# Eighteen products of the identity with itself in the first chunk of a recurrent layer with two gated layers behind it

## The chip, the cores and the metric

The kernel runs on one core of a Trainium2 chip. The metric is the device time of one launch in microseconds (us), taken as the median of several runs. The engines are named as in the profile: PE is TensorE (PEld its weight loads), DVE is VectorE, ACT is ScalarE, POOL is GpSimd, SP is SyncE, which issues most of the transfers.

## The reference

Three layers follow each other. The first is a recurrence over 768 steps for 4 batches of 8 heads, with a 40x40 state per head; the other two are gated layers over the 3072 resulting rows of 320 numbers.

```python
for t in range(S):                       # B=4, H=8, S=768, D=40
    y[:, :, t] = einsum('bhd,bhde->bhe', rt, state)
    Sa = einsum('bhde,bhe->bhd', state, at)
    state = state * wt[:, :, None, :] - einsum('bhd,bhe->bhde', Sa, bt) \
            + einsum('bhd,bhe->bhde', vt, kt)
...
g = x @ w_gate                           # 3072 x 320 times 320 x 1536
x = (g * sigmoid(g)) * (x @ w_val) @ w_out
gate = sigmoid(x @ w2_gate)
x = gate * (x @ w2_val) @ w2_out
```

## The kernel before, in words

The recurrence is cut into 12 chunks of 64 steps. For a chunk the kernel scales its inputs by running products of the decay, multiplies keys with keys (`kps`), inverts a triangular 64x64 matrix for each of the 32 pairs of batch and head, carries the state through the chunk (`qps`, `ups`, `sps`), and forms the outputs (`aps`, `yps`). `prep_a` does the first two of these, `prep_b` the inverse, `chain` the state, `post` the outputs. The work of neighbouring chunks and the first gated layer of earlier chunks is mixed by `merge`, which draws from generators by fixed rates; a scheduler then sets the order of each engine's instructions from its own estimate of time. On the chip each engine works through its list.

In the first three chunks the inverse is built in steps by `halves`. Seven sums on DVE (L567 multiplies, L573 adds) give the inverses of 16-row blocks. A first group of 64 small products on PE (`hps`, L588) is copied by ACT (L596) and goes into a second group of 64 (L601). DVE and ACT copy that result into the matrix (L617, L615), DVE turns it (L619), and then `prep_b` does the last level with `zps` and `xps` (L647).

Two other strands run beside this. The first gated layer's weights come in pieces (`raw`). Each piece goes through ACT (L1008), POOL (L1011), four steps on DVE (L1014, L1015, L1019, L1020), a cast on ACT (L1030) and two or three steps on POOL (L1032 to L1038); pieces of 384 columns and of 320 follow each other. And `powers` makes the running products of the decay for chunks 4 to 7. DVE clamps the decays (L240), which is held back until the turned copy (L619) of chunk 1 is done; POOL then makes 21 steps (L237), 14 of them on `wp`. DVE takes the reciprocal of the last of these (L257), and POOL goes on with `wq`. The results go to memory and come back for chunk 4.

The first gated layer for chunk 0 starts as soon as three of its twelve weight slices are there. It writes its two products into one PSUM bank, `gv`. DVE multiplies them into `g` (L1117), and PE writes the bank again for the next slice only after that.

A matrix product of 32-bit floats is recorded as two matmuls, so a group that the order calls x4 is x8 in the trace; transposes are recorded once.

Of the kernel before, what the change touches and what calls it, by code (L numbers as in the profile page):

```python
# [9 lines left out]
F32 = mybir.dt.float32  # L10
# [4 lines left out]
ALU = mybir.AluOpType  # L15
AX = mybir.AxisListType
PSUM = bass.MemoryType.PSUM
DRAM = bass.MemoryType.DRAM
P = 128
# [20 lines left out]
F_HIGH = (1.875 - 2.0**-23) * 2.0**16  # L40


def attention(ctx, tc, st, ident, ins, banks, extra, early, more):

# [1 line left out]
    nc = tc.nc  # L48
# [6 lines left out]
    room, fills = {}, []  # L55
# [63 lines left out]
    def tied(mats, gates):  # L119
        for x, ys, c in [(mats[0], gates, "Sync"), *((x, mats[:1], "NoSync") for x in mats[1:])]:  # L120
            for y in ys:
                tc.add_manual_dep(
                    x.ins,
                    y.ins.name,
                    mybir.DependencyInfo(getattr(mybir.DependencyClass, c), mybir.DependencyReason.DATA),
                    reason="one group",
                )
# [90 lines left out]
    inv, done, out = {}, set(), {}  # L218
# [3 lines left out]
    groups = [list(range(x, y)) for x, y in zip(cuts, cuts[1:])]  # L222
# [57 lines left out]
    for hs in HALF:  # L280
        nc.gpsimd.affine_select(
            out=mask[hs, :],
# [263 lines left out]
    def halves(m, X, bn, ps):  # L546
        t = wk.tile([P, 32 * 32], F32, tag="sn", name="sn", bufs=1)
        full = t[:, 0:512].rearrange("p (t s) -> p t s", s=32)
        sn = t[:, 512:768].rearrange("p (t s) -> p t s", s=16)
        nt = t[:, 768:896].rearrange("p (t s) -> p t s", s=16)  # L550
        t = wk.tile([P, 15 * 2 * 30], F32, tag="pr", name="pr")
        pr, turned, zt = t, t[:, 0:512].rearrange("p (t q g) -> p t q g", q=NS, g=2), t[:, 512:768]
        zt = zt.rearrange("p (q r) -> p q r", r=16)
        nc.vector.transpose(out=full, in_=walk(bn[:], 0, (1, 16), (C, NS), (16, 2)))
        nc.scalar.mul(out=sn, in_=full[:, :, 0:16], mul=par[:, 0:1])
        nc.vector.scalar_tensor_tensor(
            out=sn, in0=full[:, :, 16:32], scalar=par[:, 1:2], in1=sn, op0=ALU.mult, op1=ALU.add
        )
        nk = sn.rearrange("p t s -> p (t s)")[:, 16:256:34]
        ev, od = sn[:, 0:16:2], sn[:, 1:16:2]  # L560
        nc.scalar.mul(out=x16.rearrange("p r t -> p (r t)")[:, 1:256:34], in_=nk, mul=-1.0)
        nc.vector.tensor_tensor(out=nt, in0=ev, in1=nk[:, :, None].to_broadcast([P, 8, 16]), op=ALU.mult)
        nc.vector.tensor_tensor(out=od, in0=od, in1=nt, op=ALU.add)
        for kk in range(1, 8):
            n = 2 * kk
            o = pr[:, 0 : 2 * n * n].rearrange("p (r u s) -> p r u s", u=2, s=n)
            nc.vector.tensor_tensor(  # L567
                out=o,
                in0=x16[:, 0:n, None, 0:n].to_broadcast([P, n, 2, n]),
                in1=sn[:, None, n : n + 2, 0:n].to_broadcast([P, n, 2, n]),  # L570
                op=ALU.mult,
            )
            nc.vector.tensor_reduce(out=x16[:, 0:n, n : n + 2], in_=o, axis=AX.X, op=ALU.add)  # L573
            if kk in (3, 5):
                yield
        rows = wk.tile([P, 16, NS, 2], F32, tag="x1t", name="x1t")
        flat = lambda x: x.rearrange("p a q g -> p (a q g)")
        nc.vector.transpose(out=flat(rows), in_=walk(x16[:], 0, (16, 16), (0, 2), (1, 16)))
        nc.vector.transpose(out=flat(turned), in_=walk(x16[:], 0, (1, 16), (0, 2), (16, 16)))
        for z in range(2):  # L580
            src = turned[:, :, :, z].rearrange("p t q -> p q t")
            to = lambda l: X[:, :, 32 * l + 16 * z : 32 * l + 16 * z + 16]
            nc.scalar.mul(out=to(1), in_=src, mul=sel[:, 2 + z : 3 + z])
            nc.vector.tensor_scalar(out=to(0), in0=src, scalar1=sel[:, z : z + 1], scalar2=None, op0=ALU.mult)
        yield
        for q in range(NS):
            for j in range(4):
                nc.tensor.matmul(  # L588
                    ps[QUAD[j], q, 0:16],
                    lhsT=bn[32 * j : 32 * j + 16, q, 0:32],  # L590
                    rhs=rows[32 * j : 32 * j + 16, :, q, 0],
                    start=True,
                    stop=True,
                    tile_position=(32 * j, 32 * j),
                )
        nc.scalar.copy(out=zt, in_=ps[:, :, 0:16])  # L596
        yield
        for q in range(NS):
            for j in range(4):
                at = 32 * (j % 2) + 16  # L600
                last = nc.tensor.matmul(  # L601
                    ps[32 * j : 32 * j + 16, q, 16:32],
                    lhsT=zt[QUAD[j], q],
                    rhs=X[QUAD[j], q, at : at + 16],
                    start=True,
                    stop=True,
                    tile_position=(32 * j, 32 * j),
                )
        if m == 0:
            marks["joined"] = last  # L610
        for j in (0, 2, 1, 3):
            at = 32 * (j % 2) + 16
            to, src = X[32 * j : 32 * j + 16, :, at : at + 16], ps[32 * j : 32 * j + 16, :, 16:32]
            if j % 2:
                nc.scalar.mul(out=to, in_=src, mul=-1.0)  # L615
            else:
                nc.vector.tensor_scalar(out=to, in0=src, scalar1=-1.0, scalar2=None, op0=ALU.mult)  # L617
        x1t = wk.tile([P, NS, 32], F32, tag="x1t", name="x1t")
        last = nc.vector.transpose(out=x1t, in_=walk(X[:], 0, (C, NS), (1, 32)))  # L619
        if m == 1:  # L620
            marks["turned"] = last
        yield x1t.rearrange("p q (r g) -> p r q g", g=2)

    def prep_b(m):
        X = xinv[m % 2]
        while m not in inv:
            yield
        bn = inv.pop(m)
        pool, tag = (po, f"po{m}") if m < 2 else (pmm, "mm")
        if m < FEW:  # L630
            ps = pool.tile([P, NS, 32], F32, tag=tag, name="hps")
            steps = halves(m, X, bn, ps)
        else:
            steps = whole(m, X, bn)
        for x1t in steps:
            yield

        zt = wk.tile([P, NS, 32], F32, tag="zt", name="zt")
        for n in range(2):
            ps = pool.tile([P, NS, 32], F32, tag=tag, name="zx"[n] + "ps")  # L640
            mats = []
            for q in range(NS):
                for h2 in range(2):
                    with group(m, not mats):
                        lo, hi = slice(64 * h2, 64 * h2 + 32), slice(64 * h2 + 32, 64 * h2 + 64)
                        mats.append(
                            nc.tensor.matmul(  # L647
                                ps[(hi, lo)[n], q],
                                lhsT=(bn[lo, q, 32:64], zt[hi, q])[n],
                                rhs=(x1t[lo, :, q], X[hi, q, 32:64])[n],  # L650
                                start=True,
                                stop=True,
                                tile_position=(64 * h2 + 32 * n, 64 * h2 + 32 - 32 * n),
                            )
                        )
            if m >= FEW:
                tied(mats, copied if n else [])
            copied = []
            for h2 in range(2):
                lo, hi = slice(64 * h2, 64 * h2 + 32), slice(64 * h2 + 32, 64 * h2 + 64)  # L660
                if n:
                    nc.scalar.mul(out=X[lo, :, 32:64], in_=ps[lo], mul=-1.0)
                else:
                    copied.append(nc.scalar.copy(out=zt[hi], in_=ps[hi]))
            yield
        if m == 0:
            marks["merged"] = mats[-1]
# [177 lines left out]
    def post(m):  # L845
# [4 lines left out]
        for bp in range(2):  # L850
# [49 lines left out]
                            )  # L900
            if m >= FEW:
                tied(mats, masked)
            ysb = wk.tile([P, DM + 64], F32, tag="ysb", name="ysb", bufs=3)
            yf, pf = yps.rearrange("p h d -> p (h d)"), pn[:, DM * bp : DM * bp + DM]
            freed[:] = [
# [418 lines left out]
def rwkv_moe_kernel(ctx, tc, r, k, v, w, a, b, aw0, aw, aa, akb, av, avt, art, w1a, w2a, out):  # L1324
# [11 lines left out]
    with ExitStack() as c1:  # L1336
# [8 lines left out]
        with ExitStack() as c2:  # L1345
# [10 lines left out]
            def more(new, spare):  # L1356
# [5 lines left out]
                for tag in new[:n]:  # L1362
                    tags.append(tag)
                    yield from ffn.load_w(st, tag, layers[0], len(w1))
                    w1.append(ffn.w)

            def fills(fs, after=None):
                for f in fs:
                    yield from ffn.load_w(*first[f], layers[0], f, after)
                    w1.append(ffn.w)  # L1370
# [13 lines left out]
                        nc.sync.dma_start(out=xs[1][2 * m + u], in_=ob)  # L1384
                        yield

            attention(c2, tc, st, ident, (aw0, aw, aa, akb, av, avt, art), banks, extra, fills, more)

        with ExitStack() as c2:
            pool2 = lambda n, b, **kw: c2.enter_context(tc.tile_pool(name=n, bufs=b, **kw))  # L1390
# [166 lines left out]
```

## Time and profile before

| | |
|---|---|
| time before, median of 3 runs | 1271.05 us (1270.66 to 1273.36) |
| the profiled execution | 1274.74 us |
| its span, first to last instruction | 1272.7 us |
| PE busy | 1185.2 us (93%) |
| PEld busy | 1070.1 us (84%) |
| DVE busy | 687.8 us (54%) |
| ACT busy | 592.3 us (47%) |
| POOL busy | 557.7 us (44%) |
| mean granted TensorE clock | 0.956 of full speed |

A granted clock of 1.00 is 2.4 GHz, and 0.50 is 1.2 GHz; a stretch with a value between has some of both. Times in the rows are from the start of the span. A row of the timeline gives start, length, engine, line, operation, what is written from what, shapes and count, and in brackets the idle time before it with what ended that.

### The profile page before, as it was taken

Reading aid. Unit: us, or ns where it says so; the run is one execution under the profiler, and the core shown is the slowest. Engines: PE = TensorE matmul, PEld = TensorE weight load, DVE = VectorE, ACT = ScalarE, POOL = GpSimd, SP = SyncE. Lnnn points to the kernel's source line nnn. Section 1 sums busy time; section 2 is a strip of 40 time slices with the busy share of each in tenths; the row PEclk is TensorE's granted clock in tenths of the full one; section 3 lists DMA queues with packets and bytes.
Section 4 is the critical chain, followed back from the end, with each engine's and each line's share of the span. In section 5 each row is a group of like instructions: output and inputs, shape, how many; then the busy total and the mean of one; then the engine's idle time right before and its main releaser. Section 6 shows DMA issues by size and latency. Waiting matters only on the chain.

```text
span 1272.7 us, 31392 instructions
## 1 busy us (share of the span) xinstructions
PE 1185.2 (93%) x12545; PEld 1070.1 (84%) x12545; DVE 687.8 (54%) x1432; ACT 592.3 (47%) x1447; POOL 557.7 (44%) x749
## 2 busy tenths in 40 slices
PE   5598799999999999899999999999999999999997
PEld 4487588889889988788898888888888888888886
DVE  6867769876678667956867544467121212121111
ACT  8465546556655575455433433445232323232222
POOL 5744842233223224356855766676232223222221
PEclk8678868999999999999999999999999999999998
DMA  7444664544655555343464543323010101000001
GB/s 221 131 131 148 146 168 123 123 99 111 153 121 115 115 136 122 88 106 110 125 237 126 182 160 127 107 88 91 2 46 1 46 1 35 1 21 1 22 1 25
DMA packets 180460, 124.38 MB, mean 98 GB/s; under 512 B 134608, under 2 KB 160208, under 8 KB 179536
## 3 DMA queue, kind: packets, MB, share of 16 engines
q1 hardware_dynamic: 180144, 122.11, 35.5%
q8 instruction: 101, 1.65, 0.5%
q14 instruction: 55, 0.45, 0.1%
q10 hardware_dynamic: 160, 0.16, 0.1%
HBM read 90.81 MB, written 31.43 MB: 96 GB/s over the span
## 4 chain that ended last, share of the span: by engine, by line
PE 60%; DVE 22%; ACT 8%; issue 4%; DMA 2%; POOL 2%; SPq 0%; DVEq 0%; ACTq 0%; POOLq 0%
PE g L1167 31%; PE po L1128 16%; DVE pr L526 4%; PE gv L1112 4%; DVE part L532 3%; PE kps L486 2%; PE aps L861 2%; PE tp L371 2%; DVE lq L498 1%; PE ups L787 1%; ACT bn L496 1%; DVE am L870 1%; DVE dt L1015 1%; ACT bn L495 1%; ACT part L751 1%
## 5 line engine op out<-in xcount | busy, mean ns | idle before, releaser
L1167 PE MATMUL g<-x,w 128*128 128x512 f32 (+1 forms) x1792 | 419.8, 385 | 2.1 <-DVE g L1174 2.0
L1167 PEld LDWEIGHTS g<-x,w 128*128 128x128 f32 x1792 | 323.3, 188 | 62.8 <-issue 2.8
L1176 POOL TENSOR_TENSOR hl<-g,hh 128x256 fp32r<-128x256 f32 x216 | 162.1, 756 | 281.8 <-ACT hh L1175 253.9
L1174 DVE TENSOR_TENSOR g<-g,g 128x256 f32<-128x256 f32 x216 | 82.1, 419 | 342.4 <-PE g L1167 340.1
L1128 PE MATMUL po<-w,hh 128*128 128x320 f32 x1152 | 233.6, 311 | 0.9 <-ACT hh L1118 0.8
L1128 PEld LDWEIGHTS po<-w,hh 128*128 128x128 f32 x1152 | 187.0, 188 | 9.9 <-ACT hh L1118 1.0
L1175 ACT CAST hh<-g 128x256 fp32r<-128x256 f32 x216 | 86.9, 406 | 179.4 <-PE po L1128 169.7
L1112 PE MATMUL gv<-x,w 128*128 128x256 f32 x1152 | 165.6, 291 | 3.8 <-DVE g L1117 2.5
L1128 PE MATMUL po<-w,hl 128*128 128x320 f32 x576 | 151.1, 313 | 3.6 <-POOL hl L1119 3.5
L1112 PEld LDWEIGHTS gv<-x,w 128*128 128x128 f32 x1152 | 147.7, 192 | 6.8 <-DVE g L1117 3.9
L1171 ACT ACTIVATE g<-g 128x256 f32<-128x256 f32 x216 | 73.0, 382 | 149.5 <-PE g L1167 143.1
L1119 POOL TENSOR_TENSOR hl<-g,hh 128x256 fp32r<-128x256 f32 x72 | 62.8, 872 | 128.8 <-ACT hh L1118 127.9
L1032 POOL TENSOR_TENSOR dt<-dt,w 128x384 f32<-128x384 f32 (+1 forms) x72 | 80.3, 1116 | 87.5 <-ACT w L1030 42.7
L1128 PEld LDWEIGHTS po<-w,hl 128*128 128x128 f32 x576 | 99.6, 188 | 5.6 <-POOL hl L1119 5.2
L498 DVE TENSOR_TENSOR lq<-kps,part 64x256 f32<-64x256 f32 x96 | 40.5, 422 | 85.9 <-ACT bn L496 67.0
L526 DVE TENSOR_TENSOR pr<-part,sn 128x4 f32<-128x4 f32 (+4 forms) x135 | 76.2, 565 | 3.7
L1014 DVE TENSOR_SCALAR dt<-dt 128x384 int32<-128x384 int32 (+1 forms) x72 | 41.8, 580 | 52.8 <-POOL dt L1011 52.5
L486 PE MATMUL kps<-lq,kbt 104*128 104x128 f32 x384 | 61.3, 309 | 8.9 <-DVE lq L498 6.4
L532 DVE TENSOR_REDUCE part<-pr 128x2 f32<-128x4 f32 (+4 forms) x135 | 66.6, 493 | 2.8
L486 PEld LDWEIGHTS kps<-lq,kbt 104*128 104x128 f32 x384 | 53.4, 215 | 13.2 <-PE yps L892 4.1
L861 PE MATMUL aps<-rbd,ut 104*128 104x128 f32 x384 | 57.1, 295 | 6.1 <-DVE ysb L906 3.6
L1030 ACT CAST w<-dt 128x384 fp32r<-128x384 f32 (+1 forms) x72 | 35.6, 495 | 55.3 <-DVE dt L1015 48.2
(185 smaller groups left out, 1711.4 us busy)
## 6 DMA issues: line engine op xcount, KB each, us to landing
raw<-in_w_dram SPq DMA_DIRECT2D x48, 384.0 KB
xd<-x SPq DMA_DIRECT2D x12, 896.0 KB
x<-xd SPq DMA_DIRECT2D x11, 896.0 KB
raw<-in_w_dram SPq DMA_DIRECT2D x24, 320.0 KB
ld<-in_a_kb_dram SPq DMA_DIRECT2D x22, 320.0 KB
ld<-rd SPq DMA_DIRECT2D x64, 80.0 KB
pn<-pd SPq DMA_DIRECT2D x32, 160.0 KB
ld<-in_a_a_dram SPq DMA_DIRECT2D x12, 320.0 KB
```

The lines of the kernel that those rows point to most:

```text
L486: nc.tensor.matmul(kps[:, n].rearrange("p h t -> p (h t)"), lhsT=kbt[0:PW, n, :], rhs=lq[m % 3][0:PW, 4 * g4 + n].rearrange("p h t -> p (h ...
L526: nc.vector.tensor_tensor(out=o, in0=xs[:, 0:kk, None, 0:n].to_broadcast([P, kk, 2, n]), in1=sn[:, None, n : n + 2, 0:n].to_broadcast([P, ...
L532: nc.vector.tensor_reduce(out=xs[:, 0:kk, n : n + 2], in_=o, axis=AX.X, op=ALU.add)
L861: nc.tensor.matmul(aps[:, n, h2], lhsT=ut[0:PW, x, 2 * h2 : 2 * h2 + 2].rearrange("p u s -> p (u s)"), rhs=rbd[0:PW, x, h2].rearrange("p b ...
L1032: sub(out=tf, in0=tf, in1=w.bitcast(F32), op=ALU.subtract)
L1112: nc.tensor.matmul(gv[n], lhsT=p, rhs=q, start=e == 0, stop=e == len(seq) - 1)
L1128: self.nc.tensor.matmul(ops[u], lhsT=p[:, us], rhs=q, start=first and n == 0, stop=last and n == 2)
L1167: nc.tensor.matmul(gv[k][:, 0:n], lhsT=p, rhs=cols(at), start=e == 0, stop=e == len(seq) - 1)
L1171: nc.scalar.activation(out=g[j], in_=gv[0][:, j], func=AF.Silu if silu else AF.Sigmoid)
L1174: nc.vector.tensor_tensor(out=g[j], in0=gv[1][:, j], in1=g[j], op=ALU.mult)
L1175: nc.scalar.copy(out=hh, in_=g[j])
L1176: self.heng.tensor_tensor(out=hl, in0=g[j], in1=hh.bitcast(F32), op=ALU.subtract)
```

## The change

A function `warm` is added. It issues n products of the 128x128 identity with four copies of itself side by side, which are 512 columns, into a fresh tile of the `gv` bank. Nothing reads them. The first is made to follow a given instruction, and each of the others the one before it. It is called at five places, all in chunk 0: eight products behind the fourth sum of `halves` (with a wait on DVE for that sum), three behind the first group of `hps`, two behind the second, one behind `zps`, and four behind the first `yps`.

```diff
+            red = nc.vector.tensor_reduce(out=x16[:, 0:n, n : n + 2], in_=o, axis=AX.X, op=ALU.add)
+            if m == 0 and kk == 4:
+                warm(red, 8, "Sync")
...
         nc.scalar.copy(out=zt, in_=ps[:, :, 0:16])
+        if m == 0:
+            warm(last, 3)
...
             marks["joined"] = last
+            warm(last, 2)
...
+            if n == m == 0:
+                warm(mats[-1], 1)
...
+            if m == bp == 0:
+                warm(mats[-1], 4)
...
+            def warm(inst, n, kind="NoSync"):
+                pool, tag = ffn.pg[0]
+                to = pool.tile([P, 4, P], F32, tag=tag, name="gv")
+                wide = ident[:, None, :].to_broadcast([P, 4, P])
+                with tc.high_priority(2000):
+                    for _ in range(n):
+                        mm = nc.tensor.matmul(to, lhsT=ident, rhs=wide, start=True, stop=True)
+                        tc.add_manual_dep(mm.ins, inst.ins.name, ...)
+                        inst, kind = mm, "NoSync"
```

The scheduler places these products and then lays out the rest anew, so other instructions move as well. In the changed kernel all lines behind the first edit have higher numbers: L588, L601, L647 are now L590, L605, L652; L617, L619 are L622, L624; L1014 to L1020 are L1023 to L1029; L1117 is L1126; the products are L1382.

On PE, around the inverse of chunk 0, the new list reads as follows (`gv<-ident` are the products, `tp` transposes of chunk 1's keys):

```order
L1382 MATMUL gv<-ident 128x512 x8
L590 MATMUL hps<-x1t,bn 32x16 x64
L1382 MATMUL gv<-ident 128x512 x3
L605 MATMUL hps<-part_212,pr 16x16 x64
L1382 MATMUL gv<-ident 128x512 x2
L371 MATMUL tp<-ident,tkb_90 104x128 x8
L652 MATMUL zps<-x1t,bn 32x32 x32
L1382 MATMUL gv<-ident 128x512
L486 MATMUL kps<-lq_210,kbt 128x128 x4
```

Without the four rows of products this is the list of before as well.

On DVE, at the same place, the list of before has the copy of the second group (`hps`) and its turn behind one weight piece of 384 columns (`dt_1453`) and ahead of the next (`dt_1490`):

```order
L1014 TENSOR_SCALAR dt_1453<-dt_1453 128x384
L1015 SCALAR_TENSOR_TENSOR dt_1453<-raw_1451,dt_1453 128x384
L1019 TENSOR_SCALAR ds_1454<-dt_1453 128x384
L1020 SCALAR_TENSOR_TENSOR ds_1454<-raw_1451,ds_1454 128x384
L617 TENSOR_SCALAR part1_212<-hps_325 16x16x16 x2
L619 STREAM_TRANSPOSE x1t_536<-part1_212 128x512
L1014 TENSOR_SCALAR dt_1490<-dt_1490 128x384
```

In the new list both pieces of 384 columns (`dt_1476`, `dt_1513`) stand ahead of them:

```order
L1023 TENSOR_SCALAR dt_1476<-dt_1476 128x384
L1024 SCALAR_TENSOR_TENSOR dt_1476<-raw_1474,dt_1476 128x384
L1028 TENSOR_SCALAR ds_1477<-dt_1476 128x384
L1029 SCALAR_TENSOR_TENSOR ds_1477<-raw_1474,ds_1477 128x384
L1023 TENSOR_SCALAR dt_1513<-dt_1513 128x384
L1024 SCALAR_TENSOR_TENSOR dt_1513<-raw_1511,dt_1513 128x384
L1028 TENSOR_SCALAR ds_1514<-dt_1513 128x384
L1029 SCALAR_TENSOR_TENSOR ds_1514<-raw_1511,ds_1514 128x384
L622 TENSOR_SCALAR part1_212<-hps_325 16x16x16 x2
L624 STREAM_TRANSPOSE x1t_552<-part1_212 128x512
```

The copy and the turn have moved behind four instructions of a weight piece.

On DVE, some 80 instructions later, the list of before goes from chunk 2's last key products (`lq2`) straight to chunk 2's inverse (`sn`) and to the first gated layer's `g`; the reciprocal (L257) stands 30 instructions further on:

```order
L498 TENSOR_TENSOR lq2_211<-kps_1362,part2_86 64x4x64 x2
L554 STREAM_TRANSPOSE sn_1838<-bn_1300 128x512
L418 TENSOR_TENSOR part0_88<-ld_1713,dtp_1725 128x8x2x32
L1117 TENSOR_TENSOR g_1642<-gv_1625,g_1642 128x256
L556 SCALAR_TENSOR_TENSOR sn_1838<-sn_1838,part2_86 128x256
```

In the new list the reciprocal of the last of POOL's `wp` stands ahead of them:

```order
L1079 TENSOR_TENSOR x_1628<-xtp_1636,x_1628 64x256
L498 TENSOR_TENSOR lq2_211<-kps_1385,part2_86 64x4x64
L257 RECIPROCAL part2_86<-wp_1506 128x40
L498 TENSOR_TENSOR lq2_211<-kps_1385,part2_86 64x4x64
L554 STREAM_TRANSPOSE sn_1861<-bn_1323 128x512
L556 SCALAR_TENSOR_TENSOR sn_1861<-sn_1861,part2_86 128x256
L1126 TENSOR_TENSOR g_1665<-gv_1648,g_1665 128x256
```

The reciprocal has moved ahead of chunk 2's inverse and of the first `g`.

## Rows read from the trace of the kernel before

**Rows 1.** Busy time of each engine by stretch: start:end, length, busy (count), clock, DMA.
```profile
60.00:82.00 22.00, 21.43 (x326) 18.78 (x313) 9.82 (x21) 15.24 (x36) 12.22 (x16) 0.52 0.59 166
82.00:94.00 12.00, 11.14 (x216) 10.28 (x210) 11.74 (x29) 7.34 (x17) 4.32 (x7) 1.00 0.26 80
99.00:104.00 5.00, 4.99 (x30) 4.19 (x30) 5.00 (x13) 2.41 (x5) 0.00 (x0) 0.50 0.78 230
128.30:158.40 30.10, 22.70 (x242) 18.36 (x242) 22.09 (x46) 17.36 (x43) 23.94 (x32) 0.90 0.61 145
158.40:170.60 12.20, 12.20 (x142) 11.75 (x141) 5.44 (x11) 8.00 (x18) 4.48 (x7) 0.68 0.74 230
173.00:200.00 27.00, 25.66 (x432) 23.36 (x433) 21.06 (x49) 10.83 (x25) 12.21 (x18) 0.50 0.66 163
260.00:520.00 260.00, 249.46 (x4188) 233.88 (x4186) 196.74 (x401) 157.63 (x386) 81.69 (x96) 1.00 0.51 117
```

**Rows 2.** Timeline of PE, around the inverse of chunk 0.
```profile
54.16 1.90 PE L588 MATMUL hps<-x1t,bn 16*32 16x16 f32 x128 [9.13 <-DVE x1t L578]
...
62.33 2.19 PE L647 MATMUL zps<-x1t,bn 32*32 32x32 f32 x64 [0.26 <-ACT part L615]
...
70.55 2.05 PE L486 MATMUL kps<-lq,kbt 104*128 104x128 f32 x8 [0.31 <-DVE lq L498]
...
82.10 1.16 PE L486 MATMUL kps<-lq,kbt 104*128 104x128 f32 x8
```

**Rows 3.** Timeline of DVE: the fourth sum, and the copies behind the second group.
```profile
47.47 0.29 DVE L573 TENSOR_REDUCE x<-pr 128x16 f32<-128x128 f32 x1
...
60.55 0.84 DVE L617 TENSOR_SCALAR part<-hps 16x256 f32<-16x256 f32 x2
61.43 0.71 DVE L619 STREAM_TRANSPOSE x1t<-part 128x512 f32<-128x512 f32 x1
65.67 1.00 DVE L1014 TENSOR_SCALAR dt<-dt 128x384 int32<-128x384 int32 x1 [3.53 <-POOL dt L1011]
...
68.25 0.56 DVE L1020 SCALAR_TENSOR_TENSOR ds<-raw,ds 128x384 f32<-128x384 uint32 x1
```

**Rows 4.** Timeline of POOL, at the same place.
```profile
62.96 0.44 POOL L1036 TENSOR_TENSOR w<-dt,ds 64x128 fp32r<-64x128 f32 x1
...
65.13 0.51 POOL L1011 TENSOR_SCALAR dt<-dt 128x384 f32<-128x384 f32 x1
```

**Rows 5.** The page's part 5: the nearest row with 512 columns.
```profile
L1167 PE MATMUL g<-x,w 128*128 128x512 f32 (+1 forms) x1792 | 419.8, 385 | 2.1 <-DVE g L1174 2.0
```

**Rows 6.** Timeline of DVE, from the clamps to the reciprocal.
```profile
117.25 1.45 DVE L240 TENSOR_SCALAR wp<-wq 128x2560 f32<-128x2560 f32 x1
...
126.34 1.04 DVE L554 STREAM_TRANSPOSE sn<-bn 128x512 f32<-128x512 f32 x1
...
127.88 0.41 DVE L1117 TENSOR_TENSOR g<-gv,g 128x256 f32<-128x256 f32 x1
...
141.92 0.39 DVE L257 RECIPROCAL part<-wp 128x40 f32<-128x40 f32 x1
```

**Rows 7.** Timeline of POOL: the first and the last of the 14 steps on wp.
```profile
118.84 0.86 POOL L237 TENSOR_TENSOR wp<-wp 128x320 f32<-128x320 f32 x1 [3.42 <-issue]
...
139.84 0.86 POOL L237 TENSOR_TENSOR wp<-wp 128x320 f32<-128x320 f32 x1
```

**Rows 8.** Timeline of PE, from the second slice of the gated layer on.
```profile
128.34 2.17 PE L1112 MATMUL gv<-x,w 128*128 128x256 f32 x16 [0.83 <-DVE g L1117]
...
146.60 1.16 PE L486 MATMUL kps<-lq,kbt 104*128 104x128 f32 x8
...
158.44 2.27 PE L692 MATMUL qps<-part,lq 128*64 128x40 f32 x32
```

**Rows 9.** Timeline of ACT, where it waits for a transfer.
```profile
149.41 0.51 ACT L1030 CAST w<-dt 128x384 fp32r<-128x384 f32 x1 [2.31 <-DMA pd<-wp]
149.82 0.37 ACT L495 ACTIVATE bn<-kps 32x256 f32<-32x256 f32 x1
```

More of the change, by code (lines that the diff above doesn't have):

```diff
@@ L40, with attention @@
 F_HIGH = (1.875 - 2.0**-23) * 2.0**16
-def attention(ctx, tc, st, ident, ins, banks, extra, early, more):
+def attention(ctx, tc, st, ident, ins, banks, extra, early, more, warm):
     nc = tc.nc
@@ L572, in halves @@
             )
-            nc.vector.tensor_reduce(out=x16[:, 0:n, n : n + 2], in_=o, axis=AX.X, op=ALU.add)
+            red = nc.vector.tensor_reduce(out=x16[:, 0:n, n : n + 2], in_=o, axis=AX.X, op=ALU.add)
+            if m == 0 and kk == 4:
+                warm(red, 8, "Sync")
             if kk in (3, 5):
@@ L587, in halves @@
             for j in range(4):
-                nc.tensor.matmul(
+                last = nc.tensor.matmul(
                     ps[QUAD[j], q, 0:16],
@@ L1365, in more @@
                     w1.append(ffn.w)
+            def warm(inst, n, kind="NoSync"):
[5 more added lines that the diff above has]
+                        mm = nc.tensor.matmul(to, lhsT=ident, rhs=wide, start=True, stop=True)
+                        tc.add_manual_dep(
+                            mm.ins,
+                            inst.ins.name,
+                            mybir.DependencyInfo(
+                                getattr(mybir.DependencyClass, kind), mybir.DependencyReason.DATA
+                            ),
+                            reason="products between groups",
+                        )
+                        inst, kind = mm, "NoSync"
             def fills(fs, after=None):
@@ L1385, in extra @@
                         yield
-            attention(c2, tc, st, ident, (aw0, aw, aa, akb, av, avt, art), banks, extra, fills, more)
+            attention(c2, tc, st, ident, (aw0, aw, aa, akb, av, avt, art), banks, extra, fills, more, warm)
         with ExitStack() as c2:
```

## The prediction, as it was made before the result was known

> **What bounds the kernel now.** I read the busy time by stretch first, then the timelines of PE, DVE, POOL and ACT in the stretches where PE's clock is low or PE waits. From 260 to 520 us PE is busy 249.46 of 260 us at the granted clock 1.00 (2.4 GHz), and its share stays as high to the end [rows 1]: there PE's own work is the bound, so what the first 200 us gain or lose is carried to the end. In those first 200 us PE is not the only bound. The inverse of chunk 0 leaves PE idle for 9.13 us before the first small group [rows 2], and from 60 to 82 us PE is busy 21.43 of 22 us at the clock 0.52, almost all of it at 1.2 GHz [rows 1]. The same four key products take 2.05 us there and 1.16 us at 82.10, when the clock is back [rows 2]. From 82 to 94 us DVE is full, 11.74 of 12 us [rows 1]. A second long stretch at 0.50 lies at 173 to 200 us, PE busy 25.66 of 27 and DVE 21.06 [rows 1].
>
> **The products themselves.** No row shows such a product. It has 512 columns, as many as the four key products together, so 1.16 us at full and 2.05 at half clock bound it from above [rows 2]; below stands a recorded matmul with 512 columns, 385 ns [rows 5]. The key products are the nearer row; since their overlap counts, I take 1.0 and 2.0. Eighteen are 18 to 36 us of PE. The eight begin when the fourth sum ends, at 47.8 [rows 3]. If the clock rises after three of them, they end at 47.8 + 6 + 5 = 58.8; hps then starts 4.6 us later than 54.16. At once full, they would end at 55.8, and never raised, at 63.8. With hps at 1.3, three products, the second group at 1.2, two products and eight transposes at 1.0, PE is done with all that at 58.8 + 1.3 + 3 + 1.2 + 2 + 1 = 67.3.
>
> **First step: zps of chunk 0 waits for DVE.** In the new order DVE's copies of the second group stand behind a second weight piece. That piece can't come earlier than in the trace: POOL frees its buffer at 62.96 + 0.44 = 63.40 and takes it up at 65.13 behind two steps on wq [rows 4]; the new list has one such step of 0.86 [rows 7] less ahead of it, so 63.40 + 0.86 + 0.51 = 64.8. DVE's four steps took 65.67 to 68.81 [rows 3], which is 3.14 us; so 68.0. Then the copy (0.84, and ACT's share after it, another 0.84 by DVE's row) to 69.7, and zps at 69.8 instead of 62.33: 7.5 us late. PE has been idle since 67.3 by then, since 62 to 64 if the eight run faster. The shortest delay is 6.5 us, if each of the four steps takes no more than the last one's 0.56 [rows 3]; the longest is set by products that stay at half clock: 63.8 + 1.9 + 6 + 1.9 + 4 + 2 = 79.6, then 17 us late. I take 7.5, since every term but the clock is a row.
>
> Here a rule of the Trainium skill bears on the step. The trace shows ACT holding a cast for a transfer until 149.41 and running the next instruction, which PE had released at 146.60 + 1.16 = 147.76, only at 149.82 [rows 8, 9]. "TensorE: Matmul & The Clock Gate", section "Architectural detail: the array is 16× 32×32, not 1× 128×128", says that PE alone can pull something ahead in its queue and that ScalarE and VectorE are strict first in, first out. The trace agrees for ACT. By that rule a copy on DVE can't pass the weight piece; if it could, zps would start at 67.3 and the delay would be 5.0 instead of 7.5 us.
>
> **Second step: what the clock gives back behind it.** PE waits again before zps, so I let zps, the one product and the key products behind it run at half clock: 2.2 + 2.0 + 2.0, to 76.0. The product and the key products are dense, so I take the clock as full from there. From xps to the end of sps PE needed 82.1 - 66.4 = 15.7 us at half clock (zps at 62.33, its 2.1 and the key products' 2.0 put xps at 66.4) [rows 2]; with the ratio 1.16/2.05 that is 8.9, and the hand-overs through ACT, which was busy 15.24 of 22 us there [rows 1], add an estimated 2.4. So sps ends at 87.3 instead of 82.1: 5.2 late, 2.3 regained. With no gain it would be 7.5 + 2 late, with the clock full from zps on 2.5.
>
> **Third step: chunk 1.** From the end of sps to the clamps of the decay at 117.25 [rows 6] it is 35.1 us, mostly DVE's [rows 1]. The four products behind yps fill a wait, and the 5.0 us of PE at half clock at 99 to 104 [rows 1] can give back 2.5; less DVE work between chunk 1's sums may give another 1. I take 3.5 of at most 5: the clamps come 1.7 us late, at 118.9.
>
> **Fourth step: the reciprocal.** POOL's 14 steps on wp, with those on wq between them, end at 139.84 + 0.86 = 140.7 [rows 7], 23.4 us after the clamps began [rows 6]. In the old order DVE did chunk 2's inverse and the first g meanwhile. In the new order the reciprocal stands ahead of both, so DVE holds until 118.9 + 23.4 = 142.3. Then 0.39 for it, 0.4 for the key mask, and 1.54 from sn to g [rows 6]: g starts at 144.7 instead of 127.88. PE's second slice needs the bank that g reads, so it starts at 145.2 instead of 128.34 [rows 8]: 16.9 late. Much of that is absorbed: from 128.3 to 158.4 PE was busy 22.70 of 30.1 us, and a fifth of the stretch was at half clock [rows 1]. Without the waits, and 2 us less for the clock, 20.7 are left, so the state's next products, qps, start at 165.9 instead of 158.44: 7.5 late. Its bounds are 5.5 (only 18.7 left) and 16.9 (nothing absorbed). The next 12.2 us are full at the clock 0.68 [rows 1], of which about 7.8 at half; dense work just ahead should hold the clock, and 3 of at most 3.9 come back: 4.5 late at 170.6.
>
> **Fifth step: 173 to 200 us.** At full clock PE could save 12 of its 25.66 us, DVE's 21.06 allow 6 [rows 1]. In the new list PE has chunk 4's transposes, which wait for POOL, behind four dense products instead of ahead of them. I take a quarter of the 6: 1.5. It leaves 3.0 us, and behind it PE's own work carries it on.
>
> **Sum.** 7.5 - 2.3 - 3.5 + 15.2 - 9.4 - 3.0 - 1.5 = +3.0 us on the profiled execution's 1274.74, which lies 3.69 above the median of the runs, 1271.05. So 1274 us.
>
> **Rivals.**
> The clock holds and wins. Place: zps at about 69.8 finds PE still at 2.4 GHz, since its last product ended only a few us before, and 173 to 200 goes down to DVE's bound. For it speak the two long stretches at half clock; against it that both DVE holds stay. Time: zps, product and key products save 2.2 x 0.43 + 1 + 0.9 = 2.8, the fifth step 4.5 more, so 3.0 - 7.3 = -4.3; if the fourth step's absorption goes to its bound, another 2 (and 2 from a faster start of the eight): -8. I put it at 1265. It decides once the gains reach 3 us.
>
> It cancels. The terms above are each sure to 2 us or so and have both signs; the fourth step's absorption 3 us better than I took gives 1271, no change.
>
> The products don't do what they are there for: the clock stays at half through all fourteen of the inverse. Then zps comes 17 us late, 9.5 more than in the sum, of which the reciprocal hides little, since the clamps move along. Some 2 come back in waits: 1282. Against it: key products of the same kind run at full clock at 82.10 [rows 2], behind 20 us of mixed work.
>
> **How the numbers follow.** Forecast (slower by a few us, 1272 to 1280 on its own) 0.38; cancels 0.24; the clock wins 0.31; no clock 0.07. A run tells a difference from none at about 0.2%, 2.5 us. So faster 0.31, same 0.24, slower 0.38 + 0.07 = 0.45. The range goes to 1262 below (the clock case's -8 and 1 more) and 1282 above.
>
> **What would show it.** On DVE, L1023 to L1029 with an idle time of some 4 us before them and the copies L622 at about 68; zps at 69 to 70; the reciprocal L257 on DVE with 10 us or so of idle time released by POOL, and PE idle as long before the second slice. It would be wrong if DVE reaches the reciprocal only after POOL, if zps starts before 66, or if the clock is 1.00 from 60 to 82 and from 173 to 200: then the kernel is faster.

## The result, and the profile after

The changed kernel takes 1282.47 us, median of 6 runs (1279.56 to 1287.86), against 1271.40 us (1269.71 to 1273.36) for 6 runs of the kernel before on the same chip: ratio 1.0093, 95% interval 1.0068 to 1.0118. It is 11.1 us slower, in the direction of the forecast and just outside its range. The profiled execution took 1287.86 us, 13.1 more than that of before; its span is 1286.0 us, 13.3 more.

Busy time by stretch, after (the stretches of [rows 1], and one more, 70 to 90):
```profile
60.00:82.00 22.00, 17.71 (x309) 13.12 (x309) 7.93 (x16) 9.19 (x20) 11.97 (x16) 0.73 0.55 164
82.00:94.00 12.00, 11.68 (x157) 10.13 (x154) 5.96 (x14) 8.98 (x23) 2.65 (x4) 0.64 0.28 86
70.00:90.00 20.00, 20.00 (x255) 17.11 (x256) 5.50 (x13) 12.68 (x29) 5.90 (x9) 0.50 0.58 184
99.00:104.00 5.00, 5.00 (x88) 3.72 (x85) 4.93 (x18) 1.55 (x4) 1.81 (x3) 1.00 0.07 16
128.30:158.40 30.10, 27.82 (x280) 24.51 (x281) 14.12 (x32) 13.12 (x31) 25.69 (x33) 0.66 0.41 103
158.40:170.60 12.20, 9.89 (x128) 7.96 (x127) 9.59 (x21) 8.62 (x20) 3.82 (x7) 1.00 0.91 249
173.00:200.00 27.00, 21.82 (x493) 19.97 (x495) 14.24 (x29) 15.62 (x38) 12.83 (x17) 0.81 0.43 123
260.00:520.00 260.00, 251.35 (x4206) 235.17 (x4208) 192.65 (x387) 160.17 (x394) 79.53 (x92) 1.00 0.54 125
```
From 60 to 82 the clock is 0.73 where it was 0.52, yet PE is busy for 17.71 us instead of 21.43: it waits. From 70 to 90 it is busy throughout, at the clock 0.50. Behind 260 PE is as full as before, 251.35 of 260 against 249.46, so the loss is made in the first 260 us and carried on.

Timeline of PE, after (the places of [rows 2] and [rows 8]):
```profile
48.19 9.57 PE L1382 MATMUL gv<-ident 128*128 128x512 f32 x16 [2.78 <-DVE x L573]
...
58.89 2.84 PE L1382 MATMUL gv<-ident 128*128 128x512 f32 x6
...
69.96 1.78 PE L652 MATMUL zps<-x1t,bn 32*32 32x32 f32 x64 [4.29 <-ACT part L620]
71.67 2.08 PE L1382 MATMUL gv<-ident 128*128 128x512 f32 x2
73.53 1.91 PE L486 MATMUL kps<-lq,kbt 104*128 104x128 f32 x8
...
90.41 1.14 PE L730 MATMUL sps<-part,tkb 128*40 128x40 f32 x42
...
150.56 2.57 PE L1121 MATMUL gv<-x,w 128*128 128x256 f32 x16 [2.08 <-DVE g L1126]
...
175.14 0.31 PE L699 MATMUL qps<-part,lq 128*64 128x40 f32 x2
175.78 1.76 PE L699 MATMUL qps<-part,lq 128*64 128x40 f32 x30 [0.33 <-DMA part<-in_a_v_dram]
...
185.38 1.11 PE L899 MATMUL yps<-tkb,am 128*64 128x40 f32 x32
```
Each product is two records. The eight take 9.57 us, the three 2.84 (0.95 each, full clock), and the one behind zps 2.08 (half clock). zps starts 7.63 us later than in [rows 2], and sps ends at 91.55. The second slice is 22.2 us later than in [rows 8], the qps start 16.7 us later, and the last 30 of their 32 records wait 0.33 us for a transfer of v. yps ends at 186.49, against 170.61 before.

Timeline of DVE, after (the places of [rows 3] and [rows 6]):
```profile
65.14 1.01 DVE L1023 TENSOR_SCALAR dt<-dt 128x384 int32<-128x384 int32 x1 [4.10 <-POOL dt L1020]
...
67.71 0.56 DVE L1029 SCALAR_TENSOR_TENSOR ds<-raw,ds 128x384 f32<-128x384 uint32 x1
68.18 0.84 DVE L622 TENSOR_SCALAR part<-hps 16x256 f32<-16x256 f32 x2
...
124.03 1.45 DVE L240 TENSOR_SCALAR wp<-wq 128x2560 f32<-128x2560 f32 x1
...
145.97 0.41 DVE L257 RECIPROCAL part<-wp 128x40 f32<-128x40 f32 x1 [1.73 <-POOL wp L237]
146.75 1.06 DVE L554 STREAM_TRANSPOSE sn<-bn 128x512 f32<-128x512 f32 x1
...
150.08 0.42 DVE L1126 TENSOR_TENSOR g<-gv,g 128x256 f32<-128x256 f32 x1 [0.66 <-ACT g L1125]
```
Both holds that the prediction named are here: the weight piece waits 4.10 us for POOL with the copies L622 behind it, and the reciprocal waits for POOL's last step on wp ahead of chunk 2's inverse (sn) and of the first g. But this second wait is short: DVE is idle for 1.73 us before the reciprocal, where the prediction looked for some 10, and PE for 2.08 us before the second slice.

Timeline of ACT, after:
```profile
147.84 0.51 ACT L555 ACTIVATE sn<-sn,part 128x256 f32<-128x256 f32 x1 [2.91 <-DVE sn L554]
148.37 1.28 ACT L1125 ACT_TABLE_LOAD   x1
```
Timeline of ACT, before (its step on sn came later, at 127.56):
```profile
125.98 1.28 ACT L1116 ACT_TABLE_LOAD   x1
```
ACT loads a table for its step on g, L1125 (L1116 before). Before, it did so ahead of its step on sn; now it does so behind it, and DVE's g waits for both.

Timeline of POOL, after (the end of the steps of [rows 7], and the gated layer's hl, which its second matmul reads):
```profile
140.36 5.58 POOL L237 TENSOR_TENSOR wp<-wp 128x320 f32<-128x320 f32 x6
...
151.02 0.88 POOL L1128 TENSOR_TENSOR hl<-g,hh 128x256 fp32r<-128x256 f32 x1 [0.89 <-ACT hh L1127]
...
157.08 0.74 POOL L1128 TENSOR_TENSOR hl<-g,hh 128x256 fp32r<-128x256 f32 x1 [1.53 <-ACT hh L1127]
```
Timeline of POOL, before, the same tile:
```profile
132.05 0.72 POOL L1119 TENSOR_TENSOR hl<-g,hh 128x256 fp32r<-128x256 f32 x1
...
135.39 0.73 POOL L1119 TENSOR_TENSOR hl<-g,hh 128x256 fp32r<-128x256 f32 x1
```
Before, these two stood among the steps on wp; now they stand behind the last one.

Timeline of SP, which issues the transfers, after:
```profile
145.97 3.97 SPq L269 DMA_DIRECT2D pd<-wp  x4
...
155.58 3.33 SPq L269 DMA_DIRECT2D rd<-wq  x4
...
172.16 1.14 SPq L361 DMA_DIRECT2D part<-in_a_v_dram  x2
```
Timeline of SP, before:
```profile
140.74 3.42 SPq L269 DMA_DIRECT2D pd<-wp  x4
...
154.69 1.22 SPq L361 DMA_DIRECT2D part<-in_a_v_dram  x2
...
157.66 3.77 SPq L269 DMA_DIRECT2D rd<-wq  x4
```
The loads of v, which qps needs, were issued ahead of the stores of wq; now they stand behind them and go out at 172.16 instead of 154.69. The stores have all been issued by 158.91, though. From there on other transfers stand ahead of v, and some of them wait for other engines, so the stores' place is only a part of these 17.5 us (q3 below). The prediction did not look at this queue.

### The profile page after: what moved, and what is told of

Its sections match the earlier page's. It is cut to its first block, busy times and chain, and to the rows that moved or that the text cites. A ratio compares the mean times of both kernels' runs of the same rounds, so it can differ in the third digit from the quotient of the medians.

```text
span 1286.0 us, 31463 instructions
## 1 busy us (share of the span) xinstructions
PE 1209.3 (94%) x12581; PEld 1082.2 (84%) x12581; DVE 686.1 (53%) x1432; ACT 593.7 (46%) x1447; POOL 555.4 (43%) x749
## 4 chain that ended last, share of the span: by engine, by line
PE 59%; DVE 20%; ACT 8%; issue 5%; DMA 4%; POOL 3%; SPq 0%; ACTq 0%; DVEq 0%; POOLq 0%
PE g L1176 30%; PE po L1137 16%; PE gv L1121 4%; DVE pr L526 4%; DVE part L532 3%; PE kps L486 2%; PE tp L371 1%; DMA wt<-in_a_w_dram 1%; POOL wp L237 1%; PE aps L868 1%; PE ups L794 1%; ACT bn L496 1%; ACT bn L495 1%; DVE lq L498 1%; DVE am L877 1%
## 5 line engine op out<-in xcount | busy, mean ns | idle before, releaser
L1121 PE MATMUL gv<-x,w 128*128 128x256 f32 x1152 | 168.2, 293 | 7.4 <-DVE g L1126 4.8
L1023 DVE TENSOR_SCALAR dt<-dt 128x384 int32<-128x384 int32 (+1 forms) x72 | 40.0, 556 | 50.4 <-POOL dt L1020 50.0
L1017 ACT ACTIVATE dt<-raw 128x384 f32<-128x384 f32 (+1 forms) x72 | 38.4, 533 | 49.2 <-POOL w L1045 35.1
```

Of the source, the lines that this page charges most:

```text
L1121: nc.tensor.matmul(gv[n], lhsT=p, rhs=q, start=e == 0, stop=e == len(seq) - 1)
```

## The experiments

The change does two things: it adds products, and it makes the scheduler lay out all five queues anew. In the runs whose names begin with a to d, a dependency that only fixes the order of some instructions on an engine was added, and the scheduler planned the rest again. In the runs whose names begin with p, x or q the order of every queue is given by a table of such dependencies:

```diff
+def pin(tc, text):              # a row for each engine: its instructions in order
+    for row in ...:
+        for x, y in zip(row, row[1:]):
+            tc.add_manual_dep(at[y], x, <no semaphore>, reason="order on the engine")
+pin(tc, ORDER)
```

All ratios are to the kernel before on the same chip, with 95% intervals. Lines of code shift by up to 23 against the profiles above (that of the products by up to 93).

**a_copies: the copies of chunk 0 back ahead of the weight piece, on DVE.**
```diff
+# DVE: first turn of weight piece 5 stands behind the copies L622, L624 of chunk 0
+tc.add_manual_dep(turn.ins, last.ins.name, <no semaphore>)
```


> The changed kernel with its 18 products, but DVE's copies of the second group (L622) stand ahead of the second weight piece again, as before the change. Theory 1 (the order of DVE costs, and the clock that falls in the wait before zps): zps starts at about 66 instead of 69.96 with a wait of under 1.5 us, the clock stays near 1.00, sps ends near 80 instead of 91.55; the rest shifts along, and the kernel takes about 1271 us, 11 less than the changed one. Theory 2 (the PE time of the products costs, whatever the order): zps comes earlier but the time stays within 3 us of 1282. Between them: the clock falls all the same, sps ends near 87, 1278 us.


1319.0 us, ratio 1.0363 (1.0335 to 1.0391). zps starts at 65.16, as meant, but the scheduler planned the later work worse: from 260 to 520 PE is busy for 246.42 us at 0.96, after 251.35 at 1.00. So it tells nothing of the copies, but it shows how much one dependency can move.

**b_recip and c_both: the reciprocal back behind the first g; both edits.**
```diff
+# DVE: the reciprocal L257 of chunk 2 stands behind chunk 2's turned sn and the first g
+tc.add_manual_dep(rec.ins, last.ins.name, <no semaphore>)
```


> The changed kernel, but the reciprocal of the second decay group (L257) stands behind chunk 2's first inverse steps and the first g on DVE, as before the change; chunk 0 is left as it is. Theory 1: the second slice of the first layer starts near 136 instead of 150.56, but PE was at half clock and had 5 us of idle time less there, so about half comes back: qps near 168 instead of 175.1 and 1275 us. Theory 2 (the hold is hidden behind PE's late work, the loss is all in chunk 0): qps within 2 us of 175, 1281 us.

> The changed kernel with both places of DVE's order as before the change: copies ahead of the second weight piece, reciprocal behind the first g. Theory 1: the gains of the two add up to two thirds or more, sps ends near 80, qps near 155, and with the products' PE time already behind it the kernel is faster than before the change: 1264 us. Theory 2 (products cost their PE time): 1275 to 1280 us.


b: 1284.63 us, 1.0092 (1.0067 to 1.0117), nothing won: the second slice starts at 149.82 all the same. PE is busy for all 30.10 us from 128.3 to 158.4, at the clock 0.67, and chunk 2's inverse can't start much sooner either. Timeline of DVE, b:
```profile
145.57 1.06 DVE L556 STREAM_TRANSPOSE sn<-bn 128x512 f32<-128x512 f32 x1
```
That is 1.2 us sooner than with the reciprocal ahead of it. c: 1279.98 us, 1.0065 (1.0041 to 1.0090); the second slice comes at 139.80 instead of 150.56, but the first qps wait until 164.09 for v.

**d_before_recip and d_again: the kernel before, with the reciprocal ahead.** It puts the fourth step's order on DVE into a kernel without products.
```diff
+# kernel before. DVE: chunk 2's sn and the first g stand behind the reciprocal L257
+behind(first, "rec")
```


> The kernel before, with no products, but with the reciprocal L257 of the second decay group put ahead of the first g and of chunk 2's inverse on DVE. Theory 1: DVE holds for POOL until 141 to 142, the first g starts near 143 instead of 127.88, the second slice at 144 instead of 128.34, qps 7 to 11 us late, 1277 us. Theory 2 (hidden): 1271 to 1273 us.

> The kernel before without products, only the reciprocal ahead of the first g, once more: 1270.2 us at the first time, 0.3% ahead of the kernel before. If that gain is real, 1269 to 1271 us and a ratio under 1 again; if it was chance, within 1 us of the kernel before.


1270.23 us, 0.9971 (0.9950 to 0.9991), and again 1269.81, 0.9969 (0.9950 to 0.9987). The second slice starts at 143.66, 15.3 us late, and nothing is lost. The scheduler laid out more than the reciprocal anew: it put the next sps ahead of the slice on PE, and the loads of v went out at 147.72, well ahead of the stores of wq (164.19). POOL's first hl stands behind the last step on wp here too (144.12). So a late second slice alone isn't the loss; what stands around it decides, and d doesn't show which part of that. d is the one version that is ahead of both kernels, by 0.3%.

**p0_order_alone and p1_products_alone: the change taken apart.**
```diff
 p0:  kernel before, no products
+pin(tc, ORDER)   # all five queues in the order of the changed kernel
 p1:  changed kernel, with its 18 products
+pin(tc, ORDER)   # everything else in the order of the kernel before
```


> The kernel before, without any of the 18 products, but with every engine's instructions in the order that they have in the changed kernel (all five queues, the whole program). Theory 1 (the order costs, the products themselves little): zps of chunk 0 waits for DVE until about 70, the loads of chunk 1's v stand behind the rd<-wq stores on SP as in the changed kernel, and the kernel takes 1278 to 1284 us. Theory 2 (the PE time of the products costs): about 1271 us.

> The changed kernel with its 18 products, but every other instruction on all five queues in the order of the kernel before, the products at the same neighbours. Theory 1: zps starts near 65.5 with the clock at 1.00, sps ends near 80 instead of 82.17, and 1264 to 1271 us. Theory 2 (the products cost PE time that the clock doesn't give back): 1276 to 1282 us.


The order alone: 1288.69 us, 1.0126 (1.0099 to 1.0152). The products alone: 1271.87 us, 1.0006 (0.9988 to 1.0024). So the whole loss is the order's. In p0 zps starts at 69.09 and v goes out at 174.40, about as late as in the changed kernel. That the products give some of it back (1.0126 against 1.0093) isn't shown, since the intervals overlap.

What p1 makes of the products is seen from 60 to 82 us. Busy time, p1:
```profile
60.00:82.00 22.00, 17.73 (x442) 13.59 (x440) 9.88 (x20) 14.77 (x36) 12.12 (x16) 1.00 0.59 172
```
Timeline of PE, p1:
```profile
65.76 1.20 PE L655 MATMUL zps<-x1t,bn 32*32 32x32 f32 x64
...
79.07 1.11 PE L733 MATMUL sps<-part,tkb 128*40 128x40 f32 x46
```
Timeline of DVE, p1:
```profile
80.07 0.43 DVE L501 TENSOR_TENSOR lq<-kps,part 64x256 f32<-64x256 f32 x1 [3.29 <-ACT bn L499]
...
82.17 0.99 DVE L743 TENSOR_TENSOR part<-sps,part 40x320 f32<-40x320 f32 x2
```
Timeline of DVE, before:
```profile
80.09 0.43 DVE L498 TENSOR_TENSOR lq<-kps,part 64x256 f32<-64x256 f32 x1 [4.71 <-ACT bn L496]
...
82.19 0.99 DVE L733 TENSOR_TENSOR part<-sps,part 40x320 f32<-40x320 f32 x2
```
The clock is 1.00 instead of 0.52, and sps ends at 80.18 instead of 82.17, although zps began 3.4 us later than in [rows 2]. But in both kernels DVE waits for ACT's copies until 80.1 and takes sps up at 82.2. In the kernel before, ACT had waited for PE's key products at half clock (until 79.41). In p1 ACT has its own work without a gap from 75.03 on. It got there late because the products hold back the copies of chunk 0 and, behind them, the next weight piece (67.10 on DVE, instead of 65.67). So up to here the products cost as much as the clock gives back. What the half clock would cost by itself this run doesn't show.

**x1_order_first and x2_order_later: which part of the order.** No products; the order changes over where chunk 1's inverse begins.
```diff
 x1:  kernel before
+pin(tc, ORDER)   # changed kernel's order up to there, then the order of before
 x2:  kernel before
+pin(tc, ORDER)   # order of before up to there, then the changed kernel's
```


> The kernel before, no products, every engine in the order of the changed kernel up to the first step of chunk 1's inverse on DVE (and all that this step needs or that had begun by then), and from there on in the order of the kernel before. Theory A (chunk 0's order is the cost): 1283 to 1288 us, as with the changed order throughout (1288.7). Theory B (the later order is the cost): within 4 us of 1272.

> The reverse: the kernel before, no products, in its own order up to the first step of chunk 1's inverse, and in the changed kernel's order from there on. Theory A: within 4 us of 1272. Theory B: 1280 to 1288 us.


x1: 1279.55 us, 1.0068 (1.0053 to 1.0084). x2: 1284.27 us, 1.0091 (1.0075 to 1.0107). Both parts cost, by their ratios 9 and 12 us of 1272; p0's 16 (12.6 to 19.3) is near their sum. Timeline of PE, x2:
```profile
148.10 3.78 PE L1134 MATMUL gv<-x,w 128*128 128x256 f32 x16 [8.30 <-DVE g L1139]
...
173.88 1.93 PE L695 MATMUL qps<-part,lq 128*64 128x40 f32 x30 [0.67 <-DMA part<-in_a_v_dram]
```
Without the early loss the same two holds stand, the reciprocal's with 8.30 us of PE idle, and again qps end on v.

**p4_copies_back and p5_copies_back2: the first part's hold undone, order pinned.**
```diff
 # changed kernel, pinned to its own order, but in chunk 0
 p4:  DVE   copies L622, transpose L624 ahead of the weight piece L1023 to L1029
 p5:  p4, and on ACT its copy L620 ahead of the same piece's cast L1039
```


> The changed kernel, every engine in its own order, only DVE's copies and turn of chunk 0's second group (L622, L624) put ahead of the second weight piece. Theory 1: zps starts near 65.5 instead of 69.96, the clock stays at 1.00, sps ends near 80 instead of 91.55, the clamps of the decay come near 118 instead of 124.03, 1273 us. Rival (something else of chunk 1 is as late): sps earlier, but the clamps within 2 us of 124 and 1280 us or more.

> The changed kernel, every engine in its own order, but DVE's copies and turn (L622, L624) and ACT's share of the copies (L620) of chunk 0's second group both put ahead of the second weight piece. Theory A (chunk 0's late copies and the clock that falls behind them are the main cost): zps near 65.5, the clock stays at 1.00, sps ends near 80, chunk 1's inverse begins near 88 instead of 99, and 1272 to 1276 us. Theory B (the order from chunk 1 on costs as much): zps and sps as in A, but 1279 us or more.


p4: 1287.13 us, 1.0109 (1.0086 to 1.0133). Timeline of ACT, p4 (L623 is L620 of the changed kernel):
```profile
67.59 0.51 ACT L1061 CAST w<-dt 128x384 fp32r<-128x384 f32 x1 [2.91 <-DVE dt L1046]
68.13 0.76 ACT L623 ACTIVATE part<-hps 16x256 f32<-16x256 f32 x2
```
zps still waits 3.20 us, now for this copy: ACT has the same piece ahead of it. sps ends at 91.08, after 91.55 in the changed kernel. p5: 1288.95 us, 1.0138 (1.0122 to 1.0154). zps starts at 65.81, 4.15 us sooner than in the changed kernel, and two steps on stands ACT's share of the third piece. Timeline of ACT, p5:
```profile
72.22 0.49 ACT L1039 ACTIVATE dt<-raw 128x320 f32<-128x320 f32 x1 [3.35 <-POOL w L1067]
72.73 0.59 ACT L485 COPY kbt<-tp 104x512 f32<-104x512 f32 x1
```
Timeline of PE, p5:
```profile
73.36 2.08 PE L489 MATMUL kps<-lq,kbt 104*128 104x128 f32 x8 [5.30 <-ACT kbt L485]
```
The wait is moved on, not removed, PE is at half clock again behind it, and sps ends at 92.10. So which places of the early order make up the 9 us of x1 isn't shown. Both runs are set against the changed kernel as the scheduler left it (1.0093); it wasn't run pinned to its own order without an edit.

**p2_queue: SP alone in the order of before.**
```diff
 # changed kernel, pinned to its own order, but
 SP   loads of raw weights and of v ahead of the stores rd<-wq
```


> The changed kernel, every engine in its own order, only SP's transfers in the order of the kernel before: the loads of chunk 1's v stand ahead of the four rd<-wq stores again. Theory 1 (the queue carries the delay from the late decay clamps to qps): qps starts near 165 instead of 175, 1275 us. Rival (PE's late second slice and half clock set qps): qps within 2 us of 175, 1281 us.


1294.81 us, 1.0184 (1.0158 to 1.0210), the worst of the pinned ones. The old SP order has loads of raw weights ahead that wait 15.9 us for PE, which frees their buffers later now; pd<-wp goes out at 160.88 instead of 145.97, v at 175.80. Here one queue's old order didn't fit the new orders of the others.

**q2_x2_recip, q3_x2_queue, q4_x2_both, q6_x2_three: the later part's holds undone, one by one and together.**
```diff
 # x2, but
 q2:  DVE   reciprocal L257 behind the second g
 q3:  SP    stores rd<-wq behind the loads of v
 q4:  both
 q6:  q4, and on POOL the first two hl among the last steps on wp
```


> As the run with the changed order only from chunk 1's inverse on (no products, 1284.3 us, PE idle 8.30 us for g before the second slice, qps at 172.8 waiting for v), but the reciprocal L257 of the second decay group stands behind the second g on DVE. If the reciprocal's hold is the cost: second slice near 140 instead of 148, qps near 165, 1276 us. If the loads behind the stores on SP set qps: second slice near 140, but qps within 2 us of 172.8 and 1282 us or more.

> The same run, but on SP the four rd<-wq stores of the second decay group stand behind the two loads of chunk 1's v instead of ahead of them and of ten other loads. If the queue is the cost: v is issued near 160 instead of 169.8, qps near 165, 1276 us. If the reciprocal's hold on DVE and PE is the cost: v earlier, but qps within 3 us of 172.8 and 1282 us or more.

> Both edits together: the reciprocal behind the second g, the stores behind v. If the two waits lie beside each other, each hidden by the other, only this one gains: qps near 160 to 163, 1273 to 1276 us. If a third thing binds (POOL's steps, the clock): 1280 us or more.

> As the run with the reciprocal behind the second g and the stores behind v (1285.8 us), and on POOL the first two hl steps stand among the last steps on wp instead of behind the wq steps that need the reciprocal. If POOL's place for hl was the last of three locks: the wait of 5.26 us before the first po with hl goes, sps near 155 instead of 159, qps near 168 instead of 174, 1278 to 1281 us. If chunk 1's loads on SP still set qps by their waits for DVE and ACT: qps within 2 us of 174 and 1284 us or more.


q2: 1289.12 us, 1.0122 (1.0099 to 1.0145). q3: 1285.40, 1.0094 (1.0075 to 1.0112). q4: 1285.81, 1.0103 (1.0084 to 1.0123). q6: 1280.28, 1.0079 (1.0049 to 1.0110). x2 had 1.0091. In q2 the second slice is 6 us sooner (141.99), but its second matmul then waits for POOL; in q3 v goes out at 168.67 instead of 169.79, little sooner, and in that execution the clamps of the decay had come 0.95 us sooner as well (120.70, after 121.65 in x2). Timeline of PE, q4 (po is that second matmul):
```profile
143.19 2.18 PE L1134 MATMUL gv<-x,w 128*128 128x256 f32 x16 [2.27 <-DVE g L1139]
...
151.81 0.90 PE L1150 MATMUL po<-w,hl 128*128 128x320 f32 x2 [5.26 <-POOL hl L1141]
...
174.07 1.13 PE L695 MATMUL qps<-part,lq 128*64 128x40 f32 x32
```
Timeline of PE, q6:
```profile
144.00 0.56 PE L1150 MATMUL po<-w,hl 128*128 128x320 f32 x2
...
167.69 1.13 PE L695 MATMUL qps<-part,lq 128*64 128x40 f32 x32
```
With all three undone v goes out at 164.13, and qps starts 6.4 us sooner than in q4. Not all of that is the edit's. Up to the steps on wp the two kernels have the same lists, and yet the clamps came at 120.31 in q6's execution and at 122.77 in q4's, and the second slice at 140.72 and 143.19. That leaves some 3.9 us behind the slice. From q4 to q6 the median falls by 5.5 us and the ratio by 3 us' worth (one of q6's six runs took 1289.82); the intervals overlap, so the time alone doesn't prove it, but in the trace the wait of 5.26 us for hl is gone. The place of hl undone without that of the stores wasn't run, so whether the stores matter at all isn't shown. Of x2's loss 7 us by the medians, 10 by the ratio, remain in q6; where they lie isn't settled.

**p7_fewer and p8_d_products: can the products gain anything?** 13 products (five behind the sum, then 3, 2, 1, and two behind the second sps; none behind yps), in the order of before and in that of d.
```diff
-warm(red, 8, "Sync")
+warm(red, 5, "Sync")
-warm(mats[-1], 4)   # behind yps
+warm(..., 2)        # behind chunk 0's second sps
+pin(tc, ORDER)      # p7: order of before; p8: order of d
```


> Every other instruction in the order of the kernel before, and thirteen products: five instead of eight behind the fourth sum, then three, two and one as in the change, two behind the second sps group, where PE waited 1.75 us and the clock fell in the run with 18 products, and none behind yps. If PE's clock and the wait for the eight are what is left of the products' cost: hps at 55 instead of 57.7, sps ends near 78, aps and dtp at 84 to 90 at the clock 1.00, 1266 to 1269 us. If DVE and the loads bound chunk 1 whatever PE does: 1270 to 1273 us.

> Every other instruction in the order of the run without products in which only the reciprocal was moved (1270.2 us), with thirteen products: five behind the fourth sum, three, two, one, and two behind the second sps group. If the products gain nothing because chunk 1 waits for DVE and SP and not for PE: within 2 us of 1270.2. If their gain in chunk 0 (sps 2 us earlier) is carried on: 1267 us.


p7: 1272.10 us, 0.9999 (0.9987 to 1.0011). p8: 1271.42, 0.9988 (0.9975 to 1.0002), while d without products had 0.9971. Five products raise the clock too (0.77 and 1.00 from 60 to 82), and no time is won. In p7 DVE does take sps up 1.0 us sooner (81.19), but the two products behind the second sps put PE's next key products off from 82.10 to 83.72, and by chunk 1's next key mask on DVE (85.50, after 85.62 before) the gain is gone.

## Why the prediction was wrong

The direction was right, and both moves on DVE are where the prediction put them; the size was not: +3.0 us were forecast and the profiled executions differ by 13.1. By its steps:

- **The products' price** was right: 1.0 and 2.0 us were taken, 0.95 and 2.08 measured; the eight end at 57.76, after a forecast of 58.8.
- **First step, right**: zps at 69.96, after a forecast of 69.8. The rule of the Trainium skill on which it leaned ("TensorE: Matmul & The Clock Gate", section "Architectural detail: the array is 16× 32×32, not 1× 128×128": ScalarE and VectorE are strict first in, first out) bore on ACT here as well as on DVE: in p4 ACT's copy, whose data DVE no longer held up, ran only at 68.13, behind the cast that waited until 67.59.
- **Second step, failed**: 2.3 us were to come back, and 1.8 more were lost: sps ends 9.4 us late (91.55 against 82.17), not 5.2. The clock went to half just behind the wait, within zps (0.87 from 69.90 to 70.30, 0.50 from there to 90), and the product behind zps took 2.08 us. The step had taken the clock as full from 76 on.
- **Third step, nearly**: 2.6 us came back instead of 3.5; the clamps start 6.8 us late.
- **Fourth step, the size of the delay right by luck, the absorption failed.** From the clamps to the second slice 15.4 us were lost, after a forecast of 15.2, but not in the way of the step. It had DVE idle for some 10 us before the reciprocal; the trace has 1.73, and in b the slice comes only 0.7 us sooner without the hold, as PE's work at half clock keeps it nearly as late. Only without the early loss does the hold show its price: in x2 PE is idle for 8.30 us, and q2 has the slice 6.1 us sooner. Two terms missed in opposite ways besides. POOL's last step on wp ended 21.9 us after the clamps began, not 23.4. And from sn to g it took 3.33 us, not 1.54, since ACT's step on sn (0.51 us) and its table load (1.28 us) stand between the two now. Of the 16.9 us that the slice was to be late, 9.4 were to be absorbed before qps; of the real 22.2 it was 5.5, so qps start 16.7 us late. The step took qps as bound by PE's work behind the slice. In the trace PE waits there for other engines (it is busy for 9.89 of the 12.2 us from 158.4 to 170.6), and the last of the qps wait for v besides, by 0.33 us. Around the reciprocal the new order also puts the stores of wq ahead of the loads of v on SP, and hl behind the steps on wp on POOL. Undoing the first alone wins nothing (q3); undoing the second, on top of the reciprocal and the stores, brings some 3.9 us in the trace (q6). What else keeps qps late stays open. Of the 3.0 us behind qps 0.8 came back.
- **Fifth step**: 0.4 us came back instead of 1.5 (the second yps of the stretch ends at 200.42, after 184.98 before).

The misses are +0.1, +4.1, +0.9, +0.2, +3.9, +2.2 and +1.1 (rounded, step by step, with the fourth in three parts): 12.4 on top of 3.0 is 15.4, what the kernel is late at the second yps. From there to the end 2.1 us come back, which no step foresaw. These places are read from one execution of each kernel, and q4 and q6 lie 2.5 us apart at the clamps with the same lists, so a miss of 1 us says little; the two of about 4 us are the ones that count. The deeper fault is one of outlook: the sum priced two moves on DVE and PE and let the other queues stand, where p0 shows that the order of all five, without a single product, is the whole loss. The rival in which the products don't keep the clock up came nearest in its time (1282), but by luck: the products did raise the clock, and zps came 7.6 us late, not 17. Only the half clock behind zps is as it had it.

## What to carry to other kernels

Where a scheduler lays out the program, a small addition can cost by the new order alone: compare the order of every queue, those of SP and POOL too, and pin the old order to measure the addition by itself (here 16 us for the order, nothing for the products). Undoing one of several holds can show nothing while the next stands right behind it, so undo them together before one is called innocent. Before an edit is credited with a shift in the trace, look whether the shift is there ahead of the edit already; here 2.5 of 6.4 us were. And lifting PE's clock has its price: in p1 the products put zps off by 3.4 us, the full clock made just that good, and DVE took the result up at 82.2 us either way.

## What the runs showed of the hardware

The clock rose within the eight products: it was 0.50 from 48.19 to 52 us and 1.00 from 54 on. At 0.95 each they would take 7.6 us, at 2.08 each 16.6, and they took 9.57. It was at half behind waits of 3.20 us (p4), 4.29 (the changed kernel) and 5.30 (p5), as the dense matmuls that follow show (2.07, 2.08 and 2.08 us for what takes 1.12 to 1.16 at full clock); in p4 zps itself, right behind the wait, still ran at full clock (1.20 us). And it can stay there while PE is never idle: from 70 to 90 us of the changed kernel PE was busy for 20.00 of 20 us at 0.50, with 255 records of mostly small groups.
